# Fixed places for the users of one PSUM bank in a clustered-attention and mixture kernel

## Chip, cores and metric

The kernel runs on one core of one Trainium2 chip. Its time is the device time in microseconds (us); the profile's span goes from the first to the last instruction of the program. Engines: PE is TensorE, DVE is VectorE, ACT is ScalarE, POOL is GpSimd, and SP is SyncE, whose queue issues all the DMAs here.

## What is computed

Attention for 2 batches of 8 heads, 768 tokens, 64 columns a head, in which a query sees only the keys of its own cluster; then two feed-forward blocks on the 1536 tokens.

```python
q_assign = argmax(q_n @ c_n)                 # q, k and the centroids scaled to length 1
k_assign = argmax(k_n @ c_n)                 # 16 clusters a head
mask = q_assign[:, :, :, None] == k_assign[:, :, None, :]
scores = where(mask, q @ k.T / sqrt(64), -1e9)
attn = exp(scores - max(scores)); attn = attn / (sum(attn) + 1e-9)
x = attn @ v
...
x = prelu(x @ w_in, alpha) @ w_out           # 512 -> 2048 -> 512
xn = x / rms(x) * g
out = (silu(xn @ w_gate) * (xn @ w_val)) @ w_out2   # 512 -> 1536 -> 512
```

## The kernel before

The order of the work is written out by hand. Time is cut into slots. The sixteen heads are worked two at a time, as eight pairs (0 to 7); a pair takes 12 slots, and each of its two phases (one half of the queries, 384 columns) takes 6. Slots 0 to 95 are the attention. `plan` puts each piece of work into a slot with an offset, and `slot` issues a slot's pieces in the order of their offsets, so that an engine gets its instructions in this order. No engine goes past an instruction that waits.

In each slot `st_tile` (L532 to L534) makes one tile of scores for each of the pair's heads on TensorE, into a pool of three PSUM banks, and ScalarE takes the exponential (L534). Behind an even slot's tile comes `pv_tiles`, the product with v and the row sums of two slots (L548, L553). `max_tile` (L490) makes rough scores for a phase that comes 9 slots later, and VectorE takes their maximum (L494) out of a bank pair of which there is one; in an even slot it stands at 1.5, behind `st_tile` (offset 1), in an odd slot at 0.5, ahead of it.

PSUM's small bank, the tile `ps_pr`, of which there is one as well, has these users, and each must wait until the one before has been read: `max_rows` (L517; read by ScalarE, L519), `out_sums` (L567; read by VectorE in `out_recip`, L572), `out_bcast` (L581; read by VectorE in `out_mult`, L587), `prep_oht` (L428, the one-hot columns; read by ScalarE, L429) and the two parts of `prep_sims`: part 0, the similarities (L380; read by ScalarE into `simc`, L385), and part 1, their transposes (L390; read by VectorE in `prep_scale`, L397).

While a pair is worked, the next but one or two is prepared by a table of slots, counted from the pair's own first slot: `PAIR` for pairs 4 to 7, `FOURTH` for pair 3, `THIRD` for pair 2; `SECOND` and `FIRST` serve pairs 1 and 0. The steps: `load` (L340, L342) brings `nat` (parts 0 and 1) and `raw` (parts 2 and 3), of which there is one buffer each; `prep_sq` (L350) squares on ScalarE; `prep_ss` (L364) sums on VectorE; `prep_norm` is 14 small instructions on VectorE (L315 to L328) that end in a reciprocal; `prep_hi` (L449) casts `raw` on ScalarE into a stage buffer, and `prep_lo` (L454) has GpSimd write the rest beside it; then sims, scale, the five steps of `prep_arg` and `prep_oht`. There are two stage buffers, and pairs take them by turns. From the stage, DMAs carry the operands to where TensorE reads them: `prep_dma_a` (L458), `prep_dma_oh` (L471) and `prep_dma_b` (L465 to L467). For a pair whose first slot is b they stand in slots b-12 (a and oh, both heads), b-11 (b of the first head) and b-10 (b of the second).

So with pair 6 (b = 72) the casts stand in slots 41 and 42 at offset 4, and pair 4's last `prep_dma_b`, from the same stage buffer, in slot 38 at 2.5. `out_sums`, `out_recip`, `out_bcast` and `out_mult` of a phase come 8 and 10 slots behind its first slot, so in an even slot.

Of the kernel before, what the change touches and what calls it, by code (L numbers as in the profile page):

```python
# [19 lines left out]
SLOTS = 12  # L20
LEAD = 9
PAIR = {
    "load": ((-36, 6.1), (-36, 6.2), (-33, 6.1), (-33, 6.2)),
    "sq": ((-33, 4), (-32, 4)),
    "ss": ((-32, 5), (-31, 5)),
    "norm": tuple((-31 + n // 5, 5 + (n % 5) / 10) for n in range(14)),
    "hi": ((-31, 4), (-30, 4)),
    "lo": ((-30, 4.5), (-28, 4.5)),
    "sims": ((-29, 1.7), (-28, 0.7)),
    "scale": ((-28, 0.75),),  # L30
    "arg": ((-25, 5), (-24, 5), (-23, 5), (-22, 5), (-21, 5)),
    "oht": ((-19, 1.7),),
    "load_v": ((-9, 6),),
}
# [2 lines left out]
    "load": ((-32, 6.1), (-32, 6.2), (-28, 6.1), (-28, 6.2)),  # L37
    "sq": ((-30, 4), (-29, 4)),
    "ss": ((-29, 5), (-28, 5)),
    "norm": tuple((-27 + n // 4, 5 + (n % 4) / 10) for n in range(14)),  # L40
    "hi": ((-26, 4), (-25, 4)),
    "lo": ((-25, 4.5), (-23, 4.5)),
    "sims": ((-25, 1.7), (-23, 0.7)),
    "scale": ((-23, 0.75),),
    "arg": ((-21, 5), (-20, 5), (-19, 5), (-18, 5), (-17, 5)),
    "oht": ((-15, 1.7),),
}
THIRD = {
    **PAIR,
# [3 lines left out]
    "norm": tuple((-23 + n // 5, 5.1 + (n % 5) / 10) for n in range(14)),  # L53
    "hi": ((-23, 4), (-22, 4)),
    "lo": ((-22, 4.5), (-20, 4.5)),
    "sims": ((-21, 1.7), (-19, 0.7)),
    "scale": ((-19, 0.75),),
    "arg": ((-17, 5), (-16, 5), (-15, 5), (-14, 5), (-14, 5.1)),
    "oht": ((-13, 0.7),),
    "load_v": ((-11, 6),),  # L60
}
SECOND = {
# [113 lines left out]
class Attention:  # L176
# [423 lines left out]
    def plan(self):  # L600

        ev = {}

        def at(s, o, fn, *a):
            ev.setdefault(s, []).append((o, len(ev.get(s, [])), fn, a))

        T, NF = self.T, 2 * self.NP
        for t, o, n in WARMS:
            at(t, o, self.warm, n)
        for pr in range(self.NP):  # L610
            b = SLOTS * pr
            tab = (FIRST, SECOND, THIRD, FOURTH, PAIR)[min(pr, 4)]
            for key, fn in (("load", self.load), ("sq", self.prep_sq), ("ss", self.prep_ss), ("hi", self.prep_hi),
                            ("lo", self.prep_lo), ("sims", self.prep_sims), ("scale", self.prep_scale),
                            ("norm", self.prep_norm), ("arg", self.prep_arg), ("oht", self.prep_oht),
                            ("load_v", self.load_v)):
                for n, (t, o) in enumerate(tab.get(key, ())):
                    at(b + t, o, fn, pr, n)
            h = 2 * pr
            if pr == 0:  # L620
                at(-12, -2, self.prep_dma_oh, 1)
                at(-12, -1, self.prep_dma_b, 0)
                at(-12, 1, self.prep_dma_b, 1)
            elif pr == 1:
                at(-5, 12, self.prep_dma_a, h)
                at(-4, 12, self.prep_dma_a, h + 1)
                at(-1, 12, self.prep_dma_b, h)
                at(0, 12, self.prep_dma_b, h + 1)
                at(5, 0, self.prep_dma_oh, h)
                at(5, 0, self.prep_dma_oh, h + 1)  # L630
            else:
                for e in range(2):
                    at(b - 12, 2.5, self.prep_dma_a, h + e)
                    at(b - 12, 2.5, self.prep_dma_oh, h + e)
                    at(b - 11 + e, 2.5, self.prep_dma_b, h + e)
        for ph in range(NF):
            b = T * ph
            last = ph == NF - 1
            slots = AHEAD.get(ph, [b + k - LEAD for k in range(T)])
            for k, s in enumerate(slots):  # L640
                at(s, 0.5 if s % 2 or s < 0 else 1.5, self.max_tile, ph, k)
            mid, end = slots[T // 2 - 1], slots[-1]
            if ph < DIRECT:
                at(mid, 1.6, self.max_split, ph, 0)
                at(mid + 1, 1.8, self.max_rows, ph, 0)
                at(end, 1.6, self.max_split, ph, 1)
                at(end + 1, 0.7, self.max_rows, ph, 1)
            else:
                at(end, 1.6, self.max_split, ph, None)
                at(end + 1, 0.7, self.max_rows, ph, None)  # L650
            for t in range(T):
                at(b + t, 1, self.st_tile, b + t)
                if t % 2:
                    at(b + t + 1, 2, self.pv_tiles, (b + t) // 2)
            at(b + 6, 3, self.out_evac, ph)
            at(b + (7 if last else 8), -0.5 if last else 0.6, self.out_sums, ph)
            at(b + (7 if last else 8), -0.4 if last else 0.65, self.out_recip, ph)
            at(b + (8 if last else 10), -0.3 if last else 0.6, self.out_bcast, ph)
            at(b + (8 if last else 10), -0.2 if last else 0.65, self.out_mult, ph)
            at(b + (8 if last else 12), -0.1 if last else 4, self.out_split, ph, 0)  # L660
            at(b + (8 if last else 12), 0 if last else 4.1, self.out_split, ph, 1)
        for n, (t, o) in enumerate(EARLY):
            at(t, o, *((self.early_load, n) if n < 2 else (self.moe.decode_step,)))
        for t, o, fn, *a in TAIL:
            at(T * NF + t, o, getattr(self.moe, fn), *a)
        self.ev = ev
        self.prep_end = T * (NF - 1) - LEAD - 1
        return min(ev), max(ev)
# [467 lines left out]
```

## Time and profile before

| | |
|---|---|
| median of 3 runs | 938.54 us (936.44 to 939.04) |
| the profiled execution's own time | 936.12 us |
| its span | 934.3 us, 11564 instructions |
| mean granted clock of TensorE | 0.971 |
| busy, share of the span | PE 94%, DVE 66%, ACT 35%, POOL 40% |
| chain that ended last | PE 73%, DVE 16%, ACT 4%, issue 4% |

The chain is followed back from the last instruction, at each step to what released it. A wait is idle time of an engine just before an instruction, put down to the instruction whose semaphore came last. Matmul ends are modelled, and matmuls overlap.

### The profile page before, as it was taken

To read this page: it belongs to the slowest core of one execution; us is meant where nothing else is said; L and a number is where in the kernel's file an instruction comes from. 1 tells how busy PE (TensorE), PEld (TensorE's weight loads), DVE (VectorE), ACT (ScalarE), POOL (GpSimd) and SP (SyncE) were. 2 spreads that over 40 slices of the span, in tenths; PEclk is the share of its full clock that TensorE was granted. 3 is DMA by queue.
4 is the path that set the end of the run, shared out by engine and by line. 5 is a ranking of instruction groups with operands and counts; after the bars stand their busy time and mean duration, and the time that the engine had idled before them with its cause. 6 is when DMAs were issued, how large, how long until landed. Compare 5 with 4: busy or idle time off the path is not lost.

```text
span 934.3 us, 11564 instructions
## 1 busy us (share of the span) xinstructions
PE 878.4 (94%) x4358; PEld 645.6 (69%) x4358; DVE 614.6 (66%) x928; ACT 325.6 (35%) x623; POOL 376.8 (40%) x301
## 2 busy tenths in 40 slices
PE   6788798988999998999999998999999999999998
PEld 4544455555556566878888777787788888888886
DVE  6865754645556456688878888778995738384222
ACT  3344454444445442433333334344222222221111
POOL 5211102021000053576656777423775737463111
PEclk9599898999999999999999999999999999999999
DMA  6845252726426111121211221101131302120002
GB/s 188 211 124 135 60 125 71 194 45 173 101 70 174 47 46 46 45 90 49 88 46 67 92 89 68 45 1 45 69 113 45 107 29 91 45 69 1 1 28 108
DMA packets 24279, 75.69 MB, mean 81 GB/s; under 512 B 3680, under 2 KB 4896, under 8 KB 24224
## 3 DMA queue, kind: packets, MB, share of 16 engines
q1 hardware_dynamic: 24224, 74.96, 27.6%
q8 instruction: 34, 0.56, 0.3%
q14 instruction: 21, 0.17, 0.1%
HBM read 51.46 MB, written 3.15 MB: 58 GB/s over the span
## 4 chain that ended last, share of the span: by engine, by line
PE 73%; DVE 16%; ACT 4%; issue 4%; POOL 1%; DMA 1%; SPq 0%; ACTq 0%; DVEq 0%; POOLq 0%
PE ps_st L796 23%; PE ps_mx L796 10%; PE ps_pv L796 9%; PE ps_pv L548 7%; PE ps_pr L796 4%; PE ps_mx L490 4%; PE ps_pv L553 4%; PE ps_st L532 4%; DVE dec_a L774 3%; PE ps_st L533 3%; DVE dec_a L772 2%; DVE x L898 2%; DVE mx L494 2%; PE ps_pr L581 1%; ACT op L519 1%
## 5 line engine op out<-in xcount | busy, mean ns | idle before, releaser
L494 DVE TENSOR_REDUCE mx<-ps_mx 128x1 f32<-128x768 f32 x93 | 88.8, 954 | 82.0 <-PE ps_mx L490 81.5
L856 POOL TENSOR_TENSOR gl<-v,gh 128x512 fp32r<-128x512 f32 x68 | 94.9, 1395 | 101.4 <-ACT gh L855 101.4
L534 ACT ACTIVATE p<-ps_st 128x384 f32<-128x384 f32 x192 | 84.1, 492 | 80.4 <-PE ps_st L533 79.5
L598 POOL TENSOR_TENSOR x1l<-X,x1h 128x384 fp32r<-128x384 f32 x15 | 15.0, 1002 | 225.5 <-ACT x1h L595 225.5
L796 PE MATMUL ps_st<-x1h,stage 128*128 128x512 f32 x272 | 84.3, 391 | 0.0
L774 DVE SCALAR_TENSOR_TENSOR dec_a<-raw,dec_a 128x512 uint32<-128x512 uint32 x66 | 81.7, 1238 | 2.3
L855 ACT CAST gh<-v 128x512 fp32r<-128x512 f32 x68 | 42.3, 621 | 115.0 <-DVE v L852 64.4
L548 PE MATMUL ps_pv<-p,vnat 128*64 128x384 f32 x384 | 77.0, 525 | 0.0
L852 DVE TENSOR_TENSOR v<-ps_st,t 128x512 f32<-128x512 f32 x36 | 24.8, 690 | 77.1 <-PE ps_st L796 76.9
L532 PE MATMUL ps_st<-op 128*128 128x384 f32 x192 | 73.5, 383 | 2.1 <-ACT p L534 2.1
L848 DVE SCALAR_TENSOR_TENSOR v<-v,alpha,t 128x512 f32<-128x512 f32 x45 | 44.9, 998 | 43.4 <-ACT v L847 43.4
L533 PE MATMUL ps_st<-op 82*128 82x384 f32 x192 | 67.4, 351 | 0.0
L490 PE MATMUL ps_mx<-op 80*128 80x384 f32 x186 | 56.8, 389 | 8.3 <-DVE mx L494 8.2
L782 POOL TENSOR_TENSOR dec_a<-dec_a,woh 128x512 f32<-128x512 f32 x27 | 42.8, 1586 | 43.3 <-ACT woh L785 39.8
L796 PEld LDWEIGHTS ps_st<-x1h,stage 128*128 128x128 f32 x272 | 51.0, 188 | 10.9
L490 PEld LDWEIGHTS ps_mx<-op 80*128 80x128 f32 x186 | 33.3, 205 | 36.4 <-DVE mx L494 11.7
L898 DVE TENSOR_TENSOR x<-ps_mx,x 128x1024 f32<-128x1024 f32 x36 | 43.8, 1218 | 21.6 <-PE ps_mx L796 21.6
L796 PE MATMUL ps_st<-x1h,wvh 128*128 128x512 f32 x144 | 57.0, 396 | 0.9 <-ACT t L851 0.9
L796 PE MATMUL ps_st<-x1h,wvl 128*128 128x512 f32 x144 | 56.9, 395 | 0.0
L796 PE MATMUL ps_st<-x1l,wvh 128*128 128x512 f32 x144 | 56.8, 394 | 0.0
L898 DVE TENSOR_TENSOR x<-ps_pv,x 128x1024 f32<-128x1024 f32 x35 | 42.6, 1218 | 20.4 <-PE ps_pv L796 20.2
L796 PE MATMUL ps_st<-x1l,stage 128*128 128x512 f32 x136 | 53.4, 393 | 0.5 <-POOL x1l L942 0.5
(247 smaller groups left out, 2080.7 us busy)
## 6 DMA issues: line engine op xcount, KB each, us to landing
raw<-in_moe_w_out_dram SPq DMA_DIRECT2D x28, 512.0 KB, 3.5
op<-stage SPq DMA_DIRECT2D x32, 384.0 KB, 5.6
raw<-in_moe_w_in_dram SPq DMA_DIRECT2D x15, 512.0 KB, 3.4
raw<-in_moe_w_val_dram SPq DMA_DIRECT2D x12, 512.0 KB, 3.4
raw<-in_moe_w_gate_dram SPq DMA_DIRECT2D x12, 512.0 KB, 3.5
op<-stage SPq DMA_DIRECT2D x16, 288.0 KB, 6.8
nat<-in_qn_dram SPq DMA_DIRECT2D x8, 384.0 KB, 5.3
nat<-in_kn_dram SPq DMA_DIRECT2D x8, 384.0 KB, 5.7
```

What stands on the lines that cost most here:

```text
L490: nc.tensor.matmul(ps[:, g, :self.HS], lhsT=o1[0:80, 0, t * 128:(t + 1) * 128], rhs=o1[0:80, 1, sl], start=True, stop=True)
L494: nc.vector.tensor_reduce(out=self.mx[ph][:, k:k + 1], in_=ps[:, :, :self.HS], op=ALU.max, axis=AX.XY)
L532: nc.tensor.matmul(ps, lhsT=o1[:, 1, ks], rhs=o1[:, 0, qs], start=True, stop=False)
L533: nc.tensor.matmul(ps, lhsT=o2[:, 1, ks], rhs=o2[:, 0, qs], start=False, stop=True)
L534: nc.scalar.activation(out=p[:, e], in_=ps, func=AF.Exp, scale=self.scale)
L548: nc.tensor.matmul(ps[64 * e:64 * e + 64], lhsT=self.vnat[ph // 2][:, e, t0 + y], rhs=P[y][:, e], start=t0 + y == 0, stop=t0 + y == T - 1)
L774: v.scalar_tensor_tensor(out=a, in0=top, scalar=0xC0000000, in1=a, op0=ALU.bitwise_and, op1=ALU.bitwise_or)
L782: eng.tensor_tensor(out=af, in0=af, in1=f(hi), op=ALU.subtract)
L796: self.nc.tensor.matmul(ps, lhsT=a, rhs=b, start=first and i == 0, stop=last and i == len(terms) - 1)
L848: nc.vector.scalar_tensor_tensor(out=v, in0=v, scalar=self.nalpha[:, a], in1=t, op0=ALU.mult, op1=ALU.add)
L856: nc.gpsimd.tensor_tensor(out=lo, in0=v, in1=f(hi), op=ALU.subtract)
L898: nc.vector.tensor_tensor(out=dst, in0=ps, in1=dst, op=ALU.add)
```

## The change

`out_bcast` and `out_mult` of all phases but the last move, within their slot, from offset 0.6 to 1.7, which is behind `st_tile` and the max tile. In the tables of pairs 2 to 7 the two parts of the similarities come to stand at offset 1.7 of two slots that follow each other, and `scale` behind them in the second at 5 or more. In `PAIR`, loads, squares, sums and casts move two slots ahead, the second subtraction three, the norms one, and the arg-max steps one or two ahead for the most part (the last one stays). For pair 4 and later, counted by twelve slots, the users of the small bank are then: slots 2 and 8 `out_sums`, 3 and 9 `max_rows`, 4 and 10 `out_bcast`, 5 `prep_oht`, 6 and 7 the similarities.

```diff
--- before.py
+++ after.py
@@ -20,15 +20,15 @@
 SLOTS = 12
 LEAD = 9
 PAIR = {
-    "load": ((-36, 6.1), (-36, 6.2), (-33, 6.1), (-33, 6.2)),
-    "sq": ((-33, 4), (-32, 4)),
-    "ss": ((-32, 5), (-31, 5)),
-    "norm": tuple((-31 + n // 5, 5 + (n % 5) / 10) for n in range(14)),
-    "hi": ((-31, 4), (-30, 4)),
-    "lo": ((-30, 4.5), (-28, 4.5)),
-    "sims": ((-29, 1.7), (-28, 0.7)),
-    "scale": ((-28, 0.75),),
-    "arg": ((-25, 5), (-24, 5), (-23, 5), (-22, 5), (-21, 5)),
+    "load": ((-38, 6.1), (-38, 6.2), (-35, 6.1), (-35, 6.2)),
+    "sq": ((-35, 4), (-34, 4)),
+    "ss": ((-34, 5), (-33, 5)),
+    "norm": tuple((-32 + n // 5, 5 + (n % 5) / 10) for n in range(14)),
+    "hi": ((-33, 4), (-32, 4)),
+    "lo": ((-32, 4.5), (-31, 4.5)),
+    "sims": ((-30, 1.7), (-29, 1.7)),
+    "scale": ((-29, 5.9),),
+    "arg": ((-27, 5), (-26, 5), (-25, 5), (-23, 5), (-21, 5)),
     "oht": ((-19, 1.7),),
     "load_v": ((-9, 6),),
 }
@@ -37,13 +37,13 @@
     "load": ((-32, 6.1), (-32, 6.2), (-28, 6.1), (-28, 6.2)),
     "sq": ((-30, 4), (-29, 4)),
     "ss": ((-29, 5), (-28, 5)),
-    "norm": tuple((-27 + n // 4, 5 + (n % 4) / 10) for n in range(14)),
+    "norm": tuple((-27 + n // 5, 5 + (n % 5) / 10) for n in range(14)),
     "hi": ((-26, 4), (-25, 4)),
     "lo": ((-25, 4.5), (-23, 4.5)),
-    "sims": ((-25, 1.7), (-23, 0.7)),
-    "scale": ((-23, 0.75),),
-    "arg": ((-21, 5), (-20, 5), (-19, 5), (-18, 5), (-17, 5)),
-    "oht": ((-15, 1.7),),
+    "sims": ((-25, 1.7), (-24, 1.7)),
+    "scale": ((-24, 5.1),),
+    "arg": ((-22, 5), (-21, 5), (-20, 5), (-19, 5), (-17, 5)),
+    "oht": ((-13, 1.7),),
 }
 THIRD = {
     **PAIR,
@@ -53,10 +53,10 @@
     "norm": tuple((-23 + n // 5, 5.1 + (n % 5) / 10) for n in range(14)),
     "hi": ((-23, 4), (-22, 4)),
     "lo": ((-22, 4.5), (-20, 4.5)),
-    "sims": ((-21, 1.7), (-19, 0.7)),
-    "scale": ((-19, 0.75),),
-    "arg": ((-17, 5), (-16, 5), (-15, 5), (-14, 5), (-14, 5.1)),
-    "oht": ((-13, 0.7),),
+    "sims": ((-20, 1.7), (-19, 1.7)),
+    "scale": ((-19, 5),),
+    "arg": ((-17, 5), (-16, 5), (-15, 5), (-15, 5.1), (-14, 5)),
+    "oht": ((-13, 1.7),),
     "load_v": ((-11, 6),),
 }
 SECOND = {
@@ -655,8 +655,8 @@
             at(b + 6, 3, self.out_evac, ph)
             at(b + (7 if last else 8), -0.5 if last else 0.6, self.out_sums, ph)
             at(b + (7 if last else 8), -0.4 if last else 0.65, self.out_recip, ph)
-            at(b + (8 if last else 10), -0.3 if last else 0.6, self.out_bcast, ph)
-            at(b + (8 if last else 10), -0.2 if last else 0.65, self.out_mult, ph)
+            at(b + (8 if last else 10), -0.3 if last else 1.7, self.out_bcast, ph)
+            at(b + (8 if last else 10), -0.2 if last else 1.75, self.out_mult, ph)
             at(b + (8 if last else 12), -0.1 if last else 4, self.out_split, ph, 0)
             at(b + (8 if last else 12), 0 if last else 4.1, self.out_split, ph, 1)
         for n, (t, o) in enumerate(EARLY):
```

## Rows read from the trace of the kernel before

**Rows 1.** The page: busy times of the engines, share of the span.
```profile
PE 878.4 (94%) x4358; PEld 645.6 (69%) x4358; DVE 614.6 (66%) x928; ACT 325.6 (35%) x623; POOL 376.8 (40%) x301
```

**Rows 2.** Windows, slots 35-46 and 59-70: length, busy us by engine, granted clock.
```profile
165.26:203.57 38.31, 34.92 (x225) 20.82 (x225) 21.81 (x47) 18.36 (x40) 5.54 (x4) 0.96 0.47 119
...
243.81:275.99 32.18, 31.61 (x214) 19.28 (x214) 18.18 (x32) 14.99 (x35) 2.00 (x2) 1.00 0.46 109
```

**Rows 3.** TensorE timeline, slots 39-44: start, us, instruction, [idle before <-releaser].
```profile
176.57 0.88 PE L581 MATMUL ps_pr<-idf,rs 128*64 128x128 f32 x12 [0.29 <-ACT op L519]
...
181.68 0.34 PE L532 MATMUL ps_st<-op 128*128 128x384 f32 x1
...
187.18 0.44 PE L532 MATMUL ps_st<-op 128*128 128x384 f32 x1 [0.54 <-ACT p L534]
...
190.61 0.83 PE L567 MATMUL ps_pr<-sel,ssb 128*128 128x2 f32 x6 [2.02 <-ACT simc L385]
191.69 0.90 PE L390 MATMUL ps_pr<-idf,simc 128*128 128x128 f32 x3 [0.26 <-DVE rs L572]
```

**Rows 4.** Windows at the end of slot 43; third from right is the granted clock.
```profile
188.60:191.69 3.09, 0.83 (x6) 0.74 (x6) 0.18 (x2) 1.96 (x5) 2.21 (x2) 1.00 0.00 0
191.74:195.13 3.39, 3.39 (x11) 2.56 (x13) 1.26 (x3) 0.98 (x2) 2.27 (x2) 0.50 0.00 0
```

**Rows 5.** ScalarE timeline, slots 39-44.
```profile
176.55 0.87 ACT L534 ACTIVATE p<-ps_st 128x384 f32<-128x384 f32 x2
...
185.91 0.83 ACT L449 CAST stage<-raw 128x768 fp32r<-128x768 f32 x1 [2.62 <-issue]
...
190.03 0.53 ACT L385 ACTIVATE simc<-ps_pr 128x384 f32<-128x384 f32 x1
```

**Rows 6.** TensorE timeline, slots 19-21.
```profile
107.12 0.83 PE L567 MATMUL ps_pr<-sel,ssb 128*128 128x2 f32 x6 [1.04 <-ACT simc L385]
111.76 0.90 PE L390 MATMUL ps_pr<-idf,simc 128*128 128x128 f32 x3 [3.81 <-DVE rs L572]
...
120.97 0.88 PE L581 MATMUL ps_pr<-idf,rs 128*64 128x128 f32 x12 [0.92 <-ACT oht L429]
```

**Rows 7.** SyncE queue's timeline, slots 36-40: start of issue, us of issue.
```profile
169.17 1.45 SPq L340 DMA_DIRECT2D nat<-in_qn_dram  x1
...
178.23 1.37 SPq L467 DMA_DIRECT2D op<-stage  x1
...
181.86 0.40 SPq L342 DMA_DIRECT2D raw<-in_qt_dram  x1
```

**Rows 8.** Line L467 in slot 38, then slot 50: its waiter, issue to landing.
```profile
  ACT stage L449: 2.6, 1
DMA to landing us min/median/max: 5.4/5.4/5.4
...
DMA to landing us min/median/max: 7.8/7.8/7.8
```

**Rows 9.** VectorE timeline, slot 44.
```profile
192.63 0.56 DVE L397 TENSOR_TENSOR sims<-ps_pr,n_a 128x384 f32<-128x384 f32 x1 [0.77 <-PE ps_pr L390]
```

**Rows 10.** TensorE's slot 16; line L467 of slot 14 in SyncE's queue; its issue to landing.
```profile
95.62 0.39 PE L532 MATMUL ps_st<-op 128*128 128x384 f32 x1
...
90.53 1.74 SPq L467 DMA_DIRECT2D op<-stage  x1
...
DMA to landing us min/median/max: 9.1/9.1/9.1
```

**Rows 11.** TensorE timeline, slot 10.
```profile
73.77 0.62 PE L490 MATMUL ps_mx<-op 80*128 80x384 f32 x2 [1.05 <-DVE mx L494]
```

**Rows 12.** Timelines in slot 2: VectorE, and GpSimd in the last line.
```profile
46.02 1.68 DVE L315 TENSOR_TENSOR n_a<-n_y,ss 128x24 f32<-128x24 f32 x1
...
49.51 0.18 DVE L317 SCALAR_TENSOR_TENSOR n_y<-n_a,n_y 128x24 f32<-128x24 f32 x1
...
45.84 3.60 POOL L454 TENSOR_TENSOR stage<-raw,stage 128x768 fp32r<-128x768 f32 x2 [11.24 <-DMA op<-stage]
```

## Prediction

> **What bounds the kernel now.** I read the page first: TensorE is busy for 878.4 of 934.3 us, so at most some 56 us can be won anywhere [rows 1]. Then the windows by twelve slots, the part that the tables order: the stretch with the preparation of pair 6 in it takes 38.31 us, one with no next pair to prepare 32.18 [rows 2]. The preparation's own matrix work explains about 1.2 of the 6.1 us. The rest is waiting, and TensorE's timeline says where: in slots 43 and 44 it stands still for 0.54, 2.02 and 0.26 us [rows 3], together 2.82. The last two are the small bank: the row sums (L567) may not enter it until ScalarE has copied the similarities out, and the transposes (L390) not until VectorE has read the row sums. Then the clock: it is granted in full up to 191.7 and at one half (1.2 GHz) for the next 3.4 us; before it fell TensorE had been busy for only 0.83 of 3.09 us [rows 4]. ScalarE's timeline says why the copy is late: its queue holds it behind two casts of 0.83 us, and the first of these waited 2.62 us for its data, so the copy (L385) begins at 190.03 only [rows 5]. In pair 4 the same place costs 1.04 and 3.81 us, and the one-hot transpose and the broadcast that share slots 21 and 22 another 0.92 [rows 6]; these three make 5.8.
>
> So the complaint that the change answers is real. What it can bring is what is left after the waits that the new places make.
>
> **The change part by part.** No instruction is added or taken away; all of them move.
>
> Similarities to slots 6 and 7 of a phase pair, row sums alone in slot 8. The waits of 2.02 and 0.26 go, and that of 0.54 goes with the casts that move: 2.8 us less for each of pairs 5, 6 and 7, taken from pair 6.
>
> Loads and casts two slots earlier. This is what I weigh most. The cast (prep_hi) of pair 6 writes the stage buffer that pair 4's operand DMAs (prep_dma_b) still read, the last of them L467 of slot 38. Their slots don't move. So the cast must wait for both its raw data and that read. In the trace L467 is issued at 178.23 [rows 7] and lands 5.4 us later, at 183.6, and the profile names this line as one that the cast waits for [rows 8]. That wait costs nothing of its own before, since ScalarE comes to the cast late and the raw data, issued at 181.86 [rows 7], land later still. After the change the cast stands behind the exponentials of slot 39, which end at 176.55 + 0.87 = 177.4 [rows 5]. ScalarE then waits from 177.4 to 183.6.
>
> Does L467 land earlier by then? The two loads of nat (from 169.17, [rows 7]), 384 KB each, leave the queue ahead of it, but two loads of raw, 384 KB each, are put ahead of it: raw is now issued in slot 37, between the two prep_dma_b. The bytes ahead are the same, so I keep 183.6. By the Trainium skill (DMA: Bandwidth & Descriptors, "Queues, rings and completion order") each DMA engine takes descriptors in ring order, but a later transfer may finish its writes first; by the first half the landing stays, by the second it could come somewhat sooner, and no run here shows which.
>
> What is queued behind that cast: the exponentials of slot 40. TensorE comes to the second half of st_tile(41), which needs a bank that these free, at 181.7 [rows 3]. Cast 0.83 and half a pair of exponentials about 0.5 [rows 5]: the bank is free at 185.0, a stall of 3.3 us. The second cast (0.83) then stands in front of the exponentials of slot 41, and TensorE, two half tiles and a transpose later, waits again, about 0.65.
>
> Scale next to the row sums. The scale of slot 7 must have read the bank before the row sums of slot 8 enter, and now no tile of matrix work lies between: 0.56 us of VectorE plus about 0.1 of signalling [rows 9], so 0.65.
>
> Pairs 5 to 7: 3.3 + 0.65 + 0.65 = 4.6 added, 2.8 removed, so +1.8 each, +5.4. I let the clock cancel: before, a wait of 2.02 was enough to bring it to half for a time [rows 4], and a wait of 3.3 should do it as well. The bounds of that are plus or minus half of 3.4 us, 1.7, for each pair.
>
> Pair 4. Its cast (slot 15) writes the buffer that L467 of slot 14 reads, which lands at 90.53 + 9.1 = 99.6 [rows 10]; with nat ahead of the burst, and raw held back until GpSimd has done with pair 3's, I take 98.5. Behind the cast stand the copies of max_rows in slot 16, and behind these, for the bank, the broadcast at its new place. TensorE, which begins slot 16 at 95.62 [rows 10] and would begin it somewhat sooner, comes to the broadcast near 95.9; cast 0.83 and copy 0.5 let it start at 99.9: a stall of 4.0. In slot 20 the row sums wait for a scale that stands behind a max reduction and pair 3's last arg-max step on VectorE: between 0.65 as in the other pairs and the 3.81 that the bank costs there now [rows 6], I take 2.1. Added 6.1, removed 5.8: +0.3.
>
> The broadcasts. Each moves from ahead of its slot's st_tile to behind the max tile. The 0.29 us that it waited for ScalarE's copies [rows 3] goes, but the work was what TensorE did while ScalarE caught up: with it gone the second half of st_tile waits for the exponentials behind those same copies, until 176.55 + 0.5 [rows 5], which is 0.6 us of standing still where 0.29 and 0.88 of work were. The 0.8 us come back after the max tile. Sum zero, bounds 0.3 either way for each of the 15. In slot 10 it is no zero: there the broadcast lies ahead of two max tiles that wait for VectorE until 73.77 anyway [rows 11]; moved behind them it is paid in full, less what st_tile wins: +0.6.
>
> Loads on SyncE's queue: nat is issued well ahead of its use, and nothing waits for it; prep_dma_b and load_v, behind raw now, are needed ten slots later, except for the read above. Order of arg steps: VectorE is idle between max tiles by then; nothing.
>
> Sum: +5.4 + 0.3 + 0.6 = +6.3 us. The profiled execution took 936.12 us, its span being 934.3, and the sum makes it 942.4. The median of the runs is 938.54, 2.4 above that execution, and the forecast for a median is **944.8**.
>
> **The rivals.** *The read is over in time.* If L467 landed by 180.3 (181.7 less 0.83 and 0.5), 3.3 us sooner than in the trace, ScalarE's wait would be hidden and the change would win. Then pairs 5 to 7 lose 2.8 and get the clock back (1.7), and pay the 0.65, so -3.85 each; but the GpSimd subtractions (prep_lo) would then run in the slots of the norm steps. While two of them ran in slot 2, a norm step that otherwise takes 0.18 us took 1.68, and so did the next [rows 12]; behind such steps stands the max reduction that TensorE waits for, at about 0.5 a pair. -10 for three. Pair 4 loses 5.8 and two lots of slow clock (3.4), and has 2.1 for its scale and some 0.9 for the held norm steps: -6.2. With slot 10, -15.8: 923. For it: the burst is shorter at its head, and 3.3 us are little in a queue where landing takes 5.4 to 9.1 [rows 8, 10]. Against it: equal bytes.
> By the Trainium skill (SBUF — State Buffer, "SBUF: two separate sides") GpSimd and VectorE hold a shared port by turns, each for a whole instruction; the trace agrees, 1.68 for 0.18.
>
> *Even trade.* L467 lands about 1.5 to 2 us sooner, or the clock stays up in the new waits: each takes 1.5 to 2 from every pair, and the four pairs come out at zero: 938.5. That the bank was never the bound ends here as well.
>
> *Worse.* The clock falls twice in a pair (at the hold and at the scale), 1.7 each beyond what falls now, and L467 lands as late as the 7.8 of pair 7 [rows 8], 2.4 more: 951 or above.
>
> **How the numbers follow.** Forecast 0.48, its own range 940 to 950; read over in time 0.22; even trade 0.22; worse 0.08. What a measurement of this kernel can tell from no change is about 0.3%, 2.8 us. Faster by more: 0.22 and a little of the even trade, 0.25. Within: most of the even trade and the low edge of the forecast, 0.23. Slower: 0.52. The range 922 to 953 leaves out half of the winning case (0.11) and the upper half of the worst.
>
> **What would show it.** Right, if in slots 39 to 41 of the new trace ScalarE stands idle for some 5 us ahead of the first L449 of pairs 5 to 7, TensorE's second half of st_tile(41) waits about 3.3 us for L534, and L567 in slot 44 waits about 0.65 for L397, while its waits for L385 are gone. In slot 16 the broadcast (L581) should wait some 4 us for L519. Wrong, if L449 starts right behind the exponentials of slot 39, which is the winning case, or if the stretches of [rows 2] lose more than a microsecond each.

## The result and the profile after

The changed kernel takes 944.67 us (median of 10 runs, 940.57 to 949.96), the kernel before 937.49 (933.57 to 941.04, 10 runs beside them): ratio 1.0074, 95% interval 1.0046 to 1.0101, so slower by 7 us. The forecast was 944.8. The profiled execution's span is 942.8 us, 8.5 more than before, and the mean granted clock 0.962.

TensorE's busy time over the whole span is what it was [rows 1], so the time went into standing still:

```profile
PE 878.1 (93%) x4358; PEld 646.2 (69%) x4358; DVE 609.1 (65%) x928; ACT 325.3 (35%) x623; POOL 376.9 (40%) x301
```

The windows by twelve slots say where. The lines are slots 23 to 34, 35 to 46, 47 to 58 and 59 to 70; columns as in [rows 2].

```profile
126.47:169.67 43.20, 36.77 (x229) 21.58 (x228) 20.99 (x47) 18.69 (x41) 5.84 (x5) 0.88 0.43 106
169.67:211.57 41.90, 35.78 (x225) 21.30 (x225) 21.00 (x47) 18.28 (x40) 5.62 (x4) 0.92 0.45 109
211.57:252.90 41.33, 35.40 (x225) 21.15 (x225) 20.99 (x47) 18.29 (x40) 5.62 (x4) 0.92 0.44 103
252.90:285.11 32.21, 31.31 (x214) 19.35 (x214) 16.46 (x30) 14.89 (x35) 2.01 (x2) 1.00 0.47 109
```

Pair 6's stretch is 41.90 and was 38.31; the three together are 126.43 and were 118.10. The stretch with no next pair is unchanged (32.21 against 32.18), although its two broadcasts moved as well.

TensorE's timeline of slots 41 to 43 answers to [rows 3]:

```profile
190.73 0.69 PE L532 MATMUL ps_st<-op 128*128 128x384 f32 x1 [4.49 <-ACT p L534]
...
200.85 0.80 PE L567 MATMUL ps_pr<-sel,ssb 128*128 128x2 f32 x6 [0.74 <-DVE sims L397]
```

The waits of 2.02 and 0.26 at the small bank are gone. In their place stands one of 4.49 at the second half of st_tile(41), for exponentials. ScalarE's timeline, with SyncE's queue and the landing of its line L467 below it, tells why they are late (compare [rows 5] and [rows 7, 8]):

```profile
180.95 0.87 ACT L534 ACTIVATE p<-ps_st 128x384 f32<-128x384 f32 x2
189.45 0.83 ACT L449 CAST stage<-raw 128x768 fp32r<-128x768 f32 x1 [7.63 <-DMA vnat<-in_vn_dram]
190.19 0.86 ACT L534 ACTIVATE p<-ps_st 128x384 f32<-128x384 f32 x2
190.94 0.83 ACT L449 CAST stage<-raw 128x768 fp32r<-128x768 f32 x1
```

```profile
170.04 0.67 SPq L458 DMA_DIRECT2D op<-stage  x1
...
177.61 1.85 SPq L342 DMA_DIRECT2D raw<-in_qt_dram  x1
...
181.19 0.59 SPq L467 DMA_DIRECT2D op<-stage  x1
181.88 2.67 SPq L346 DMA_DIRECT2D vnat<-in_vn_dram  x1
...
DMA to landing us min/median/max: 8.0/8.0/8.0
```

ScalarE stands in front of the cast for 7.63 us. The row puts that to a DMA of `vnat`, but the cast does not read `vnat`, and that transfer lands only at 189.9 (181.88 + 8.0), 0.4 after the cast has begun. What fits is the line before it in the queue, L467, issued at 181.19 and landed 8.0 later, at 189.2, 0.3 ahead of the cast. The two raw loads had landed by 185.9 (179.50 + 6.4 for the second), so the raw data was not what it waited for. (For the casts of pairs 4 and 7 in this kernel, and in experiments below, the profile names the read of the stage itself.) The cast holds the exponentials of slot 40, and these hold TensorE. Pairs 5 and 7 show the same, 4.80 and 4.29. Windows of the wait and of what follows it (third column from the right: granted clock):

```profile
186.20:190.70 4.50, 0.04 (x1) 0.00 (x0) 1.51 (x6) 1.25 (x3) 0.34 (x1) 0.95 0.90 277
...
190.21:197.03 6.82, 6.30 (x25) 3.73 (x27) 1.72 (x5) 4.20 (x10) 3.62 (x2) 0.50 0.04 14
```

TensorE was busy for 0.04 of 4.50 us, and then has half the clock for 6.8 us. The early slots, 10, 11, 16 and 20, in TensorE's timeline:

```profile
72.70 0.62 PE L490 MATMUL ps_mx<-op 80*128 80x384 f32 x2 [1.74 <-DVE mx L494]
80.49 0.85 PE L380 MATMUL ps_pr<-raw,cb 128*32 128x384 f32 x8 [0.92 <-ACT oht L429]
...
99.51 1.55 PE L581 MATMUL ps_pr<-idf,rs 128*64 128x128 f32 x12 [2.42 <-ACT op L519]
...
114.20 0.80 PE L567 MATMUL ps_pr<-sel,ssb 128*128 128x2 f32 x6 [2.06 <-DVE sims L397]
```

### The profile page after: what moved, and what is told of

It is laid out like the page before. It is cut to its first block, busy times and chain, and to the rows that moved or that the text cites. A ratio compares the mean times of both kernels' runs of the same rounds, so it can differ in the third digit from the quotient of the medians.

```text
span 942.8 us, 11565 instructions
## 1 busy us (share of the span) xinstructions
PE 878.1 (93%) x4358; PEld 646.2 (69%) x4358; DVE 609.1 (65%) x928; ACT 325.3 (35%) x623; POOL 376.9 (40%) x301
## 4 chain that ended last, share of the span: by engine, by line
PE 70%; DVE 16%; issue 5%; ACT 4%; DMA 3%; POOL 2%; SPq 0%; ACTq 0%; POOLq 0%; DVEq 0%
PE ps_st L796 23%; PE ps_mx L796 10%; PE ps_pv L796 9%; PE ps_pv L548 7%; PE ps_pr L796 4%; PE ps_mx L490 4%; PE ps_pv L553 4%; PE ps_st L532 3%; DVE dec_a L774 3%; PE ps_st L533 3%; DVE x L898 2%; DVE dec_a L772 2%; DMA nat<-in_qn_dram 1%; DVE mx L494 1%; PE ps_pr L581 1%
## 5 line engine op out<-in xcount | busy, mean ns | idle before, releaser
L454 POOL TENSOR_TENSOR stage<-raw,stage 128x768 fp32r<-128x768 f32 x16 | 29.0, 1825 | 93.4 <-ACT stage L449 77.8
L532 PEld LDWEIGHTS ps_st<-op 128*128 128x128 f32 x192 | 38.3, 199 | 27.7 <-ACT p L534 25.4
```

Source lines behind the costliest of these rows:

```text
L532: nc.tensor.matmul(ps, lhsT=o1[:, 1, ks], rhs=o1[:, 0, qs], start=True, stop=False)
```

## The experiments

The theory: the loss is ScalarE's cast, which must wait until the operand DMAs of two pairs before have read the stage buffer (A). Its rivals: the new places of similarities and broadcasts cost the time themselves; the clock alone; a cast in front of exponentials costs whatever it waits for. The kernel before, run beside them, had medians of 937.79 (first four), 936.56 (old places, early tables, row sums late, queue cleared) and 936.76 us (the last four); kernels of different groups are best compared by their ratios to it.

**Casts back.** The changed kernel with one edit. `PAIR` serves pair 4 as well, so that here and in most runs below its casts move too, although the expectations speak of pairs 5 to 7:

```diff
 PAIR = {
...
-    "hi": ((-33, 4), (-32, 4)),
-    "lo": ((-32, 4.5), (-31, 4.5)),
+    "hi": ((-31, 4), (-30, 4)),
+    "lo": ((-30, 4.5), (-28, 4.5)),
```

> The changed kernel with only the casts and subtractions (prep_hi, prep_lo) of pairs 5 to 7 put back two slots later, to their old places; similarities, scale, broadcasts and loads stay at the new ones. Theory A, the loss is ScalarE's cast waiting for the last prep_dma_b of two pairs before, with the exponentials behind it: the waits of 4.80, 4.49 and 4.29 us at the second half of st_tile(29), (41), (53) go, the waits for the similarities do not come back, 0.74 at the row sums stays; the three twelve-slot stretches end at or under those of before, and the whole at 932 us (927 to 937). Rival B, the new places of similarities and broadcasts cost the time themselves: 942 to 947, stretches as long as in the changed kernel. Rival C, the waits go but the half clock is what counts and stays: 937 to 941.

Measured: 916.9 us (914.32 to 925.68), ratio to before 0.9788 (0.9751 to 0.9824). The holds are gone and nothing came for them; the expectation was right in kind, 15 us too high, and its range was missed: 932 is about what the three holds alone give (944.67 less 13.58), and the clock and slots 14 to 22 came on top. The three stretches in the windows:

```profile
118.77:153.67 34.90, 33.12 (x228) 19.98 (x228) 21.27 (x47) 18.48 (x41) 5.83 (x5) 1.00 0.56 131
153.67:188.42 34.75, 32.88 (x225) 19.78 (x225) 22.45 (x47) 18.07 (x40) 5.57 (x4) 1.00 0.54 131
188.42:222.87 34.45, 32.80 (x225) 19.76 (x225) 22.23 (x47) 18.18 (x40) 5.57 (x4) 1.00 0.52 124
```

They sum to 104.10, which is 22.33 under the changed kernel. TensorE's busy time fell by 9.15 (107.95 to 98.80) with the same work in it: that is the clock, now 1.00 in all three, and 3 us a pair. The other 13.18 are waits. Slots 14 to 22, with pair 4's casts, went from 37.96 to 30.52. ScalarE's timeline, and TensorE's:

```profile
173.45 0.83 ACT L449 CAST stage<-raw 128x768 fp32r<-128x768 f32 x1 [1.75 <-DMA vnat<-in_vn_dram]
174.19 0.86 ACT L534 ACTIVATE p<-ps_st 128x384 f32<-128x384 f32 x2
```

```profile
175.68 0.34 PE L532 MATMUL ps_st<-op 128*128 128x384 f32 x1
...
177.27 0.80 PE L567 MATMUL ps_pr<-sel,ssb 128*128 128x2 f32 x6 [0.74 <-DVE sims L397]
```

The cast still waits, 1.75 us; but the half tile (the second half of a `st_tile`) that needs its followers comes at 175.68, when the first of the two exponentials from 174.19 is done. The wait is hidden by about a microsecond.

**Read first.** The second `prep_dma_b` ahead of the raw loads:

```diff
-                    at(b - 11 + e, 2.5, self.prep_dma_b, h + e)
+                    at(b - 11, 2.5, self.prep_dma_b, h + e)
```

> The changed kernel with both prep_dma_b of a pair issued in its slot -11, so that the second stands ahead of the two raw loads on SyncE's queue and not behind them. Theory A with the order of the queue deciding: the last L467 of pair 4 lands some 4.4 us sooner (189.15 less the 4.37 us between the landing of the first prep_dma_b and of the second raw load), the first raw load some 2 to 3 us later, and the cast starts when that is there, near 186.5 and not at 189.45: the holds of 4.3 to 4.8 shrink to about 1.5, pair 4's of 2.4 to near nothing, and the whole comes to 934 us (931 to 938). Rival, bytes are shared out whatever the order: holds as long as before, 942 to 947.

Measured: 937.29 us (932.3 to 943.4), ratio 0.9995 (0.9969 to 1.0021). ScalarE's cast and TensorE's half tile in slot 41, then in slot 53:

```profile
185.28 0.83 ACT L449 CAST stage<-raw 128x768 fp32r<-128x768 f32 x1 [5.77 <-issue]
```

```profile
186.55 0.44 PE L532 MATMUL ps_st<-op 128*128 128x384 f32 x1 [2.62 <-ACT p L534]
...
226.08 0.44 PE L532 MATMUL ps_st<-op 128*128 128x384 f32 x1 [1.36 <-ACT p L534]
```

L467 now lands at 182.9 (177.37 + 5.5), and the first raw load at 185.1 (178.77 + 6.3); the cast goes 0.2 behind this load. So the hold follows the transfer that comes last, and shrank to 2.90, 2.62 and 1.36, not 1.5: two thirds of the gain I expected. Pair 4's wait of 2.42 at the broadcast is gone, as expected, but slots 14 to 22 did not get shorter (39.19 at a clock of 0.78, against 37.96 at 0.87).

**Broadcasts alone**, in the kernel before:

```diff
-            at(b + (8 if last else 10), -0.3 if last else 0.6, self.out_bcast, ph)
-            at(b + (8 if last else 10), -0.2 if last else 0.65, self.out_mult, ph)
+            at(b + (8 if last else 10), -0.3 if last else 1.7, self.out_bcast, ph)
+            at(b + (8 if last else 10), -0.2 if last else 1.75, self.out_mult, ph)
```

> The kernel before with one part of the change alone: the broadcast and the multiplication behind it (out_bcast, out_mult) at 1.7 and 1.75 of their slot. My sum: nothing in 15 phases, about 0.6 us in slot 10, at most 1.7 more if TensorE's clock falls there: 938 to 940 us. Rival, the broadcasts carry the loss: some 0.5 us each, 944 or more. Rival, they gain: under 935.

Measured: 934.46 us (932.36 to 941.43), ratio 0.9958 (0.9932 to 0.9983): a small gain that I had not expected. The profiled executions do not show it (spans 933.9 and 934.3). They show slots 10 to 13 longer (18.26 against 15.99), as expected, and other stretches shorter, slots 47 to 58 above all (37.94 against 40.24); why is not shown.

**Loads and casts alone**, in the kernel before: `load`, `sq`, `ss`, `norm`, `hi` and `lo` of `PAIR` as in the changed kernel, `sims`, `scale`, `arg` and the broadcasts as before.

```diff
-    "load": ((-36, 6.1), (-36, 6.2), (-33, 6.1), (-33, 6.2)),
...
-    "hi": ((-31, 4), (-30, 4)),
-    "lo": ((-30, 4.5), (-28, 4.5)),
+    "load": ((-38, 6.1), (-38, 6.2), (-35, 6.1), (-35, 6.2)),
...
+    "hi": ((-33, 4), (-32, 4)),
+    "lo": ((-32, 4.5), (-31, 4.5)),
```

> The kernel before with one part of the change alone: loads, squares, sums, norm steps, casts and subtractions of pairs 5 to 7 two slots earlier as in the changed kernel; similarities, scale, arg-max and broadcasts at the old places. Theory A: the hold of 4 to 5 us at the second half of st_tile(41) is there as in the changed kernel, and since ScalarE has no cast in front of the copy of the similarities any more, the waits of 2.02 and most of 0.54 at the row sums and the second half go as well: +1.5 to +2 for each of three pairs, 942.5 us (940 to 946). Rival, the loss needs the new places of the bank's users: 929 to 938.

Measured: 942.82 us (940.43 to 945.62), ratio 1.0046 (1.0026 to 1.0067), as theory A had it. The loss does not need the new places of the bank's users:

```profile
186.34 0.69 PE L532 MATMUL ps_st<-op 128*128 128x384 f32 x1 [3.83 <-ACT p L534]
...
196.08 0.83 PE L567 MATMUL ps_pr<-sel,ssb 128*128 128x2 f32 x6 [0.61 <-ACT simc L385]
197.17 0.55 PE L390 MATMUL ps_pr<-idf,simc 128*128 128x128 f32 x3 [0.26 <-DVE rs L572]
```

And the 2.02 us at the row sums shrink to 0.61 without any new place: in ScalarE's timeline no cast stands in front of the copy any more, which begins at 195.54 behind a pair of exponentials.

**The queue cleared.** The changed kernel, casts where the change put them:

```diff
+FIFTH = {
+    **PAIR,
+    "load": ((-41, 6.1), (-41, 6.2), (-39, 6.1), (-39, 6.2)),
+}
...
-                    at(b - 11 + e, 2.5, self.prep_dma_b, h + e)
+                    at(b - 11, 2.5, self.prep_dma_b, h + e)
```

> The changed kernel, its casts left where the change put them (slot 39 for pair 6), but with nothing in front of the operand DMAs: both prep_dma_b of a pair in its slot -11, and for pairs 5 to 7 nat loaded in slot -41 and raw in -39, ahead of the burst. Theory A, the hold is the read and not the cast as such: without the 1.5 MB of nat and raw the last L467 lands some 11.5 us behind the burst's start, by the end of the exponentials of slot 39, and ScalarE never waits; the holds of 4.3 to 4.8 and the half clock of pairs 5 to 7 go, their stretches come to 34.7 to 35.5 us as in the kernel with the casts back; pair 4's place stays as in the changed kernel, some 7.4 more: 924.5 us (921 to 928). Rival, a cast in front of the exponentials of slot 40 costs by itself (0.83 us and the subtractions beside the norm steps): holds of 1 to 2 us stay, 932 to 940.

Measured: 930.42 us (928.04 to 931.89), ratio 0.9926 (0.9897 to 0.9954): between the two expectations. ScalarE's cast and TensorE's half tile, and the read's waiter and landing (four lines were added, so L449 is L453 and L467 is L471):

```profile
181.42 0.84 ACT L453 CAST stage<-raw 128x768 fp32r<-128x768 f32 x1 [3.80 <-DMA op<-stage]
```

```profile
182.70 0.44 PE L536 MATMUL ps_st<-op 128*128 128x384 f32 x1 [0.67 <-ACT p L538]
```

```profile
  ACT stage L453: 3.8, 1
...
DMA to landing us min/median/max: 5.6/5.6/5.6
```

Here the profile names the read. It lands at 181.1 (175.54 + 5.6), 15.3 us behind the burst's start at 165.83; in the changed kernel it was 19.2 (189.2 less 170.04). So it comes 3.9 us sooner, and the hold of 4.49 is 0.67: one for one. My 11.5 was wrong, since nat does not stand there in the changed kernel (it is issued in the gap after the burst before, and SyncE's timeline shows none between 150 and 170): only the two raw loads were to be cleared, and the operand DMAs take 15.3 with no load ahead of the last of them (a load of `vnat` is issued 1.4 behind it). The hold of 0.67, and one of 1.17 in pair 5, were each followed by a spell of half clock (147.7 to 151.2 and 185.3 to 188.7): TensorE's busy time in the three stretches is 103.02 and not 98.80, which is most of the 6 us that I missed by. A hold of 0.73 in pair 7 was not followed by half clock.

**Old places.** The kernel with the casts back, and besides:

```diff
-    "sims": ((-30, 1.7), (-29, 1.7)),
-    "scale": ((-29, 5.9),),
-    "arg": ((-27, 5), (-26, 5), (-25, 5), (-23, 5), (-21, 5)),
+    "sims": ((-29, 1.7), (-28, 0.7)),
+    "scale": ((-28, 0.75),),
+    "arg": ((-25, 5), (-24, 5), (-23, 5), (-22, 5), (-21, 5)),
```

> The kernel with the casts back, and besides the similarities, scale and arg-max steps of pairs 4 to 7 at their old places: of the change it keeps the earlier loads, squares, sums and norms, the early tables and the broadcasts. If what made it fast is raw data that is there before the casts, so that these start when the read is over, the row sums wait some 0.9 us for the copy and the read of the bank, as in the kernel with loads and casts alone, and no more; pairs 5 to 7 come to some 35 us each, pair 4 pays its waits of 1.0 and 3.8 us and half clock: 922.5 us (918 to 928). Rival, the new places of the bank are what made it fast: the waits of about 2.8 us and the half clock are back in every pair, 931 to 938.

Measured: 925.6 us (920.19 to 932.1), ratio 0.9887 (0.9844 to 0.993). TensorE in slots 43 and 44:

```profile
180.16 0.83 PE L567 MATMUL ps_pr<-sel,ssb 128*128 128x2 f32 x6 [1.25 <-ACT simc L385]
181.25 0.55 PE L390 MATMUL ps_pr<-idf,simc 128*128 128x128 f32 x3 [0.26 <-DVE rs L572]
```

The waits of [rows 3] are 1.51 and were 2.82. So of the 21 us between before and the casts-back kernel some 9 are the new places (925.6 less 916.9; the profiled spans differ by 5.9), and the larger part comes of the rest. In the rest are the earlier loads, by which the raw data is there when the cast comes (it waits 0.84 us in place of 2.62), but also the earlier squares, sums and norms, the early tables and the broadcasts; no run has the loads by themselves. The median fell into the expected range by other parts than I had: pairs 5 to 7 took 36.90, 36.86 and 35.24, two of them at a clock of 0.95, and pair 4 paid neither a wait of 3.8 nor half clock (30.88 for slots 14 to 22, at 1.00).

**Early tables back.** The kernel with the casts back, `FOURTH` and `THIRD` as before, and:

```diff
-            at(b + (8 if last else 10), -0.3 if last else 1.7, self.out_bcast, ph)
+            at(b + (8 if last else 10), -0.3 if last else 1.7 if ph else 0.6, self.out_bcast, ph)
```

> The kernel with the casts back, and besides the tables of pairs 2 and 3 as before the change and the broadcast of phase 0 ahead of st_tile again. What slots 10 to 13 lost (18.98 us against 15.99) should come back, less some 0.7 us that slots 0 to 9 then lose: 914.6 us (912 to 918) where the kernel with the casts back has 916.9. Rival, these slots only trade waits: 917 to 920.

Measured: 918.97 us (914.83 to 924.1). The median lies with the rival, but three of the six runs took 914.8 to 915.5 and three 922.5 to 924.1, so it is not decided by it. The profiled execution, with 923.95 one of the upper three, bears the rival out: slots 10 to 13 do come down to 16.05, but slots 0 to 9 take 2.3 more, so that the two together gain only 0.6.

**Row sums late.** The kernel with the casts back, and besides:

```diff
-            at(b + (7 if last else 8), -0.5 if last else 0.6, self.out_sums, ph)
-            at(b + (7 if last else 8), -0.4 if last else 0.65, self.out_recip, ph)
+            at(b + (7 if last else 8), -0.5 if last else 1.6, self.out_sums, ph)
+            at(b + (7 if last else 8), -0.4 if last else 1.65, self.out_recip, ph)
```

> The kernel with the casts back, and besides the row sums and their reciprocal (out_sums, out_recip) at 1.6 and 1.65 of their slot, behind a tile of scores and a max tile, so that VectorE's scale is over when they come. The wait of 0.74 us that pairs 5 to 7 have at L567 goes, and some of pair 4's 1.2: 914.5 us (912 to 917). Rival, the transposes of max_rows in the next slot then wait for the reciprocal instead: 916 to 919.

Measured: 921.03 us (917.22 to 923.22). The 0.74 goes, and TensorE, earlier at its half tile, waits for ScalarE instead:

```profile
182.40 0.44 PE L532 MATMUL ps_st<-op 128*128 128x384 f32 x1 [1.35 <-ACT p L534]
```

Neither of the two expectations had that: the row sums were work that TensorE did while ScalarE caught up. The stretch of slots 59 to 70 pays as well, 32.95 against 32.21. The three pairs come to 104.67 against 104.10, so most of the 8 us by which this execution is longer stands elsewhere: 3.4 in slots 14 to 22 and 2.5 behind slot 70.

**One pair.** The kernel with the casts back, with one hold put in:

```diff
+SIXTH = {**PAIR, "hi": ((-33, 4), (-32, 4)), "lo": ((-32, 4.5), (-31, 4.5))}
...
-            tab = (FIRST, SECOND, THIRD, FOURTH, PAIR)[min(pr, 4)]
+            tab = SIXTH if pr == 6 else (FIRST, SECOND, THIRD, FOURTH, PAIR)[min(pr, 4)]
```

> The kernel with the casts back, but for pair 6 alone the casts and subtractions at the changed kernel's early places: one hold. Theory A, each hold costs its wait and the slow clock after it: the wait of 4.5 us at the second half of st_tile(41) and about 2.9 us of half clock (by which TensorE's busy time in slots 35 to 46 differs between the changed kernel and the one with the casts back, 35.77 against 32.89), the other pairs as with the casts back: 916.9 + 7.4 = 924.3 us (921 to 928). Rival, the wait alone counts, the clock falls anyway: 921; or it is made good later: 917 to 919.

Measured: 929.48 us (921.38 to 930.66), ratio 0.9888 (0.9849 to 0.9928). The windows of pair 6 and of slots 14 to 22, and below them slots 14 to 22 of the kernel with the casts back:

```profile
158.74:199.74 41.00, 35.87 (x225) 21.30 (x225) 21.00 (x47) 18.27 (x40) 5.62 (x4) 0.92 0.45 111
...
88.45:123.75 35.30, 31.95 (x187) 17.64 (x187) 19.80 (x47) 13.19 (x29) 5.39 (x4) 0.85 0.28 80
```

```profile
88.25:118.77 30.52, 27.17 (x187) 15.91 (x187) 20.51 (x47) 13.06 (x29) 5.39 (x4) 1.00 0.34 93
```

The hold costs 6.25 in its own stretch (41.00 against 34.75): 3.49 of waiting at the half tile, of which some 0.2 is won back at other waits, and 2.99 of busy time at the lower clock; the neighbours are as with the casts back (34.99 and 34.46). So in its stretch the hold costs nearly what theory A said, 6.25 for 7.4, while the median is 1.5 us above the expected range. Another 4.8 of this execution lie in slots 14 to 22, where the two kernels have the same instructions and the same 3.35 us of waits, and one was granted 0.85 of the clock and the other 1.00.

**Casts one slot earlier** than in the casts-back kernel:

```diff
-    "hi": ((-31, 4), (-30, 4)),
+    "hi": ((-32, 4), (-31, 4)),
```

> The kernel with the casts back, but the casts one slot earlier (slots 40 and 41 for pair 6), half of the way to the changed kernel. Theory A: the read ends when it ends, and the cast now holds the exponentials of slot 41, which the second half of st_tile(42) needs at 171.1; they would be done at 173.45 + 0.83 + 0.49 = 174.7 (times of the kernel with the casts back, where the place one slot later needs them at 175.7 and waits for nothing): a hold of 3.6 in pairs 5 to 7, with the clock 6.5 each, and some 5 in pair 4: 941 us (935 to 945). Rival, the cost grows evenly with the slots: halfway, 930.

Measured: 937.91 us (936.94 to 943.26), ratio 1.0009 (0.9987 to 1.0031): 21 us for one slot, where two cost 28. In slot 42:

```profile
186.70 0.69 PE L532 MATMUL ps_st<-op 128*128 128x384 f32 x1 [2.96 <-ACT p L534]
```

The holds are 3.76, 2.96 and 1.83, and the three stretches 15.1 longer than with the casts back; slots 14 to 22 are 6.8 longer, where pair 4's row sums wait 5.27 for the scale. The cost does not grow evenly; three quarters of it is in the step from a hidden wait to an open one.

**Broadcasts back.** The kernel with the casts back, with the broadcasts where they were before the change:

```diff
-            at(b + (8 if last else 10), -0.3 if last else 1.7, self.out_bcast, ph)
-            at(b + (8 if last else 10), -0.2 if last else 1.75, self.out_mult, ph)
+            at(b + (8 if last else 10), -0.3 if last else 0.6, self.out_bcast, ph)
+            at(b + (8 if last else 10), -0.2 if last else 0.65, self.out_mult, ph)
```

> The kernel with the casts back, and besides all broadcasts and multiplications ahead of st_tile again (0.6 and 0.65). By my sum the move costs nothing in 15 phases and something in slot 10: 914 to 917 us. Rival, by the run of the broadcasts alone, which was 3.3 us under the kernel before: 919 to 922.

Measured: 920.48 us (917.16 to 926.03), 3.6 above the casts-back kernel (916.9), whose runs overlap with it. It points the same way as the broadcasts alone, 3 us for the move. The three pairs come out within about 0.3 us each of the casts-back kernel's. Slots 10 to 13 take 2.7 less and slots 0 to 9 2.4 more, which is nearly even, and slots 14 to 22 take 36.33 at a clock of 0.86, 5.8 more. So what the move is worth is not settled by this.

**Margin.** The kernel with the casts back, and besides:

```diff
-                    at(b - 11 + e, 2.5, self.prep_dma_b, h + e)
+                    at(b - 11, 2.5, self.prep_dma_b, h + e)
```

> The kernel with the casts back, and besides both prep_dma_b of a pair in its slot -11, ahead of the raw loads. The read then ends some 4 us sooner; but the cast's wait for it is hidden already (bank free 1 us before TensorE comes), so by theory A nothing: 915 to 919 us. Rival, the read still costs something that the one profile doesn't show: 910 to 914.

Measured: 919.62 us (914.56 to 922.85), 0.6 above the expected range, and by ratio to the kernel before (0.9794 against 0.9788) as long as with the casts back; span of the profiled execution 912.8 against 912.5. So nothing that can be told from the scatter, as theory A had it.

## Why the prediction was right

**The cast behind the read** was the mechanism, with its place and its sign: the casts back take the loss away, the loads and casts alone make it, and the hold follows the landing one for one. Its size was off. I took 3.3 and it was 4.80, 4.49 and 4.29. The step that failed is that equal bytes ahead mean an equal landing: from the start of slot 35, L467 landed after 18.4 us before (178.23 + 5.4 less 165.26) and after 19.5 now. Those 1.1 us are about the 1.2 by which pair 6's hold is longer. The second hold, taken as 0.65, did not show in the changed kernel, where TensorE is then at half clock; in the kernels with a shorter hold it is about 0.25. The two together were forecast as 3.95, and are 4.5 in pair 6. The Trainium skill (DMA: Bandwidth & Descriptors, "Queues, rings and completion order") says that a later descriptor may finish its write before an earlier one; no run here shows L467 gain from that, and in the changed kernel it landed 3.3 us behind the second of the raw loads ahead of it.

**Scale next to the row sums**: 0.65 forecast, 0.74 measured. **What was removed**, 2.8, taken from pair 6: the two waits at the bank are gone, and the 0.54 with them; in pairs 5 and 7 the three were 2.69 and 3.45.

**The clock cancels**: TensorE's busy time in the three stretches is 107.95 after and 107.46 before, the latter with 36.30, 34.92 and 36.24. So the step holds. What I did not see is its full price. I took 1.7 a pair for the clock given back; the casts-back kernel got 3 (98.80 busy, in 104.10). That is 3.6 of the 6 us between the 923 of the rival in which the read is over in time and the 916.9 measured (its sum, given as -15.8, comes to -15.6); slots 14 to 22, which fell by 7.8 where it had 6.2, are another 1.6. A hold like these costs its own length and about three on top.

**Pairs 5 to 7** lost 8.3 us and not 5.4 (3.65, 3.59 and 1.09; pair 7 had been the dearest before): 13.6 of holds and 2.2 of waits for the scale, less the 9.0 removed, and with 1.0 in the six slots of the broadcasts (a wait of 0.45 at the second half of st_tile in place of one of 0.29 at the broadcast) and 0.5 of busy time. **Pair 4** came to -0.37 for +0.3, by other parts than I had: the broadcast waited 2.42 and not 4.0, since TensorE came to it at 97.1 and not at 95.9; the row sums waited 2.06 for the scale, as forecast. **Slot 10**: the max tiles waited 0.69 longer, close to the 0.6, but the clock fell there as well, and I had left out the similarities of slot 11, which wait 0.92 for the one-hot copy; slots 10 to 13 lost 3.0, slots 0 to 9 gave 0.7 back, and what stands ahead of slot 0 another 1.2. **The other broadcasts** came to zero in the stretches, as forecast; the 3 us that the medians give for their move are not explained by it.

So the span grew by 8.5 where the sum said 6.3, and the median by 7.2. That the forecast came out within 0.2 us is luck: its base, the median of three runs, was 1 us high. The case for the loss was one that the profile bore out at each place; nothing in the change made the read end sooner, which the rival of 923 would have needed. Of its signs, ScalarE's idle time ahead of the cast (7.63 for some 5), the hold, the wait for the scale and the end of the waits for L385 came as named; the broadcast's wait of some 4 us in slot 16 came smaller.

**SBUF's shared port** cost little. In the queue-cleared kernel two norm steps run beside GpSimd's subtraction and take 1.61 and 1.75 us in place of 0.18, as in [rows 12], and TensorE shows no wait from it; I had priced it at 0.5 a pair. In the casts-back kernel it is a step of max_split (L499) that takes 1.73 us beside the subtraction in place of 0.17, and TensorE waits 0.24 behind it in pair 6. The Trainium skill (SBUF — State Buffer, "SBUF: two separate sides") has the two engines hold that port by turns, each for a whole instruction, and the trace agrees: 1.61, 1.75 and 1.73 us, where one subtraction takes about 1.8.

**Open**: why slots 14 to 22 were granted 1.00 of the clock with 3.35 us of waits (the kernels casts back and margin) and 0.85 and 0.78 with 3.35 and 3.20 (one pair, early tables back); the scatter of the casts-back kernel's runs (914 to 926) is of that size, and so differences of 1 to 4 us between the last kernels are not told apart. And the 3 us of the broadcasts.

## What to carry to other kernels

When a step that writes a shared buffer is moved earlier, look up when its last reader ends in the trace, and what stands behind the step on its own engine: here one slot, for the casts of four pairs, was the difference between a wait that costs nothing and 21 us. A change of several moves can hold a gain and a larger loss: this one, without the casts' move, is 2.1% faster than the kernel before, and 916.9 us is the lowest median found. Price a wait of TensorE with the clock that it loses behind it, from a stretch that ran at full clock, if the trace has one.

## What the runs showed of the hardware

The clock's price: 2.6 to 3.7 us of busy time for pair 5, 6 or 7 in the changed kernel over the casts-back kernel, which was granted full clock in these three stretches with waits of at most 0.74 in them. The length of a single wait did not decide it: in the queue-cleared kernel one of 0.67 was followed by half clock and one of 0.73 was not, and neither was one of 1.36 (slot 53 of the kernel that reads first, granted 1.00 in that stretch). The ten operand DMAs of a pair take 15.3 us from the start of their issue to the last landing in the queue-cleared kernel, where I had reckoned with 11.5. And the profile can name the wrong transfer: where it put the cast's wait to `vnat` in the changed kernel, that transfer landed 0.4 us after the cast had begun.
